# A strided sparse attention followed by an ELU layer: batch 2 transposed by the DMA crossbar, its P v and sums in one matmul, constants of v written first

## The chip, the cores and the metric

The kernel runs on one core of a Trainium2 chip. The core has a matrix engine (TensorE, in the profile PE, with its weight loads shown apart as PEld), a vector engine (VectorE, DVE), a scalar engine for activations (ScalarE, ACT), a general engine (GpSimd, POOL) and a sync engine (SP). Each runs its own list of instructions in order; they wait for each other through semaphores. The DMA engines move data between the chip's memory and the on-chip memory; a transfer is issued by SP, ACT or POOL. The metric is the time of one launch on the device in microseconds (us), as the median of several executions.

## What is computed

Eight batches of eight heads, 576 tokens, 64 values a head. Heads 0 to 3 attend to the last 32 tokens ("local"), heads 4 to 7 to every 32nd earlier token ("strided"). What comes out goes through two dense layers (512 to 2048 to 512) with an ELU between them.

```python
scores = scale * np.matmul(q, k.transpose(0, 1, 3, 2))
rel = pos[:, None] - pos[None, :]
mask_local = (rel >= 0) & (rel < 32)
mask_strided = (rel >= 0) & (pos[None, :] % 32 == pos[:, None] % 32)
masks = np.stack([mask_local if h < H // 2 else mask_strided for h in range(H)], axis=0)
attn = softmax(np.where(masks, scores, -1e9))
x = (attn @ v).transpose(0, 2, 1, 3).reshape(B * S, H * D)        # 4608 x 512
h = x @ w_in                                                      # 4608 x 2048
g = np.where(h > 0.0, h, np.exp(np.minimum(h, 0.0)) - 1.0)
out = g @ w_out                                                   # 4608 x 512
```

## The kernel before

**Tiling.** The tokens of a batch are cut into 8 residues of 72 tokens for the strided heads, and into 6 blocks of 96 for the local ones. Two heads make a pair, so a batch has four pairs: 0 and 1 are local, 2 and 3 strided; each pair has two halves u of 288 columns. A *piece* is one (pair, half). The result of a batch goes, transposed, into `xT` (128 x 4 x columns), a ring of 2304 columns. The dense layers go over 18 blocks j of 256 columns. `l1(j, t)` makes 256 of the 2048 hidden values: eight matmuls (line 406), an exponential on ACT (413), and on DVE a minimum (420) and a maximum (421); a "B" variant does more of it on ACT (416). `l2(j, kk, part)` is four matmuls (463), a quarter of one output tile of 128 tokens; after the last quarter ACT copies the tile to `osb` (468) and SP stores it in several transfers (451).

**A piece of attention.** `piece_S` (line 279 on) multiplies transposed keys by transposed queries into `sc` (293), ACT takes the exponential (296), and DVE multiplies by the mask (298 strided, 304 local) into `pm`. Then P v is made in one of two ways. `mm_O2` and `tail_O2` (kinds "M" and "E", or "X" for both at once) form the sums of the rows by a matmul with a tile of ones (368, 374) and P v by matmuls with 64 columns of v (378); the tail is one logarithm and one exponential on ACT (385, 387) and one product on DVE (313, 317) for 128 partitions. `piece_O` (kind "O") has v next to a block of 64 ones, so the same matmul (345) gives P v and the sums; its tail is two logarithms on 64 partitions (348, 349), one exponential (351) and two products on 64 partitions. Batches 0, 1 and 2 are done in the first way, batches 3 to 7 in the second.

**Who transposes.** q and k have to be turned so that the 64 values of a head lie on partitions. In batches 0, 1 and 2 `piece_T` does this on PE with an identity (268, 270) into a PSUM tile of the pool `p_x`, followed by two copies (253). In batches 3 to 7 `dma_T` (169) has SP issue four DMA transposes a batch: `qs` and `ks` (strided heads), `kl` and `ql` (local heads). The results lie in `qsT`, `ksT`, `klT`, `qlT`, two of each, used by turns.

**Loads.** From batch 1 on all loads of q, k and v are issued by POOL, which also casts them: `load_str` (143) one transfer for the four strided heads of a tensor, `load_kl16` (125) four transfers, `load_vl16` (133, 134) eight, `load_vsx16` (138) four, and `load_ql16` one transfer of 1024-byte rows in batches 1 and 2 (115) and four of 128-byte rows from batch 3 on (119). There is one `qs` and one `ks`: the load of the next batch into them waits until the transposes of the batch before have read them. POOL keeps to its order, and a load also waits until the eighth load before it has landed.

**Constants of v.** `vlx` and `vsx`, two of each, hold v with blocks of ones between. `one_columns(i)` writes these ones on ACT (528), for i = 0 inside batch 0 and for i = 1 after batch 0, behind a memset of `vlx[1]` on DVE (558).

**Order.** Everything is written out by hand. Batch 0 runs with matmuls on a constant between its pieces ("f"). Then come the first two blocks of the first layer (`l1_wide` at 431 to 440, and `l1`), with the strided transposes of batch 1 between them. Batch 1 follows in a list of steps, in which "2" is one quarter of `l2`, "S4" a `piece_S`, "A5" and "B4" an `mm_O2`, "E4" a `tail_O2`, "T0" a `piece_T`, "v", "k", "x" loads, and "t" the strided transposes of batch 2. The main loop counts n over `l1(j, t)`, j from 2 on; `at(n, ...)` hangs the pieces of batches 2 to 7 into it, at places given by `SC`, and `l2_to(n + 10)` puts in the quarters of `l2`. The pools that matter: `p_x` has two wide PSUM tiles (scores, P v and transposes), `p_h` three (hidden values), `p_o` one (output), and there are three `osb`.

Of the kernel before, what the change touches and what calls it, by code (L numbers as in the profile page):

```python
# [17 lines left out]
D = 64  # L18
# [12 lines left out]
def kernel(  # L31
# [44 lines left out]
    vs = const([RS, HG, NS * D], BF16, "vs")  # L76

    qlb = [const([RP, 2, NS, 2 * D], BF16, f"qlb{i}") for i in range(2)]
    qld = [t.rearrange("p a s c -> p (a s c)").rearrange("p (h c) -> p h c", h=HG) for t in qlb]
    klb = [const([LQ, 2, LB, 2 * D], BF16, f"klb{i}") for i in range(2)]  # L80
    KLW = PRE + 2 * S
    KSW = 16 * RP + 48
# [28 lines left out]


    def load_ql16(b):
        if b < 3:
            nc.gpsimd.dma_start(out=qld[b % 2][0:RS],
                                in_=q[b, 0:HG].rearrange("h (p s) d -> p h (s d)", s=NS))
            return
        for h in range(HG):
            nc.gpsimd.dma_start(  # L119
                out=qlb[b % 2][0:RS, h // 2, :, (h % 2) * D:(h % 2 + 1) * D],  # L120
                in_=q[b, h].rearrange("(p s) d -> p s d", s=NS))

    def load_kl16(b):
        for h in range(HG):
            nc.gpsimd.dma_start(  # L125
                out=klb[b % 2][:, h // 2, :, (h % 2) * D:(h % 2 + 1) * D],
                in_=k[b, h].rearrange("(t p) d -> p t d", p=LQ))

    def load_vl16(b):
        for h in range(HG):  # L130
            x = v[b, h].rearrange("(t p) d -> p t d", p=LQ)
            t = vlx[b % 2][:, h // 2, :, 2 * (h % 2) * D:(2 * (h % 2) + 1) * D]
            nc.gpsimd.dma_start(out=t[PRE:128], in_=x)  # L133
            nc.gpsimd.dma_start(out=t[0:PRE, 1:], in_=x[LQ - PRE:, 0:LB - 1, :])  # L134

    def load_vsx16(b):
        for h in range(HG):
            nc.gpsimd.dma_start(  # L138
                out=vsx[b % 2][:, h // 2, :, 2 * (h % 2) * D:(2 * (h % 2) + 1) * D],
                in_=v[b, HG + h].rearrange("(p s) d -> p s d", s=NS))  # L140

    def load_str(b, dst, src):
        nc.gpsimd.dma_start(  # L143
            out=dst[0:RS], in_=src[b, HG:2 * HG].rearrange("h (p s) d -> p h (s d)", s=NS))
# [35 lines left out]
    ones = const([128, D], BF16, "ones")  # L180
    dist = const([RS, RS], I32, "dist")
    nc.vector.memset(warm, 1.0)  # L182
    nc.vector.memset(identity, 1.0)
    nc.vector.memset(base_l, 1.0)
    for t in (qs, ks):
# [2 lines left out]
        identity, identity, compare_op=ALU.is_equal, fill=0.0,  # L188
        base=0, pattern=[[1, 128]], channel_multiplier=-1,
    )  # L190
    load_str(0, qs, q)
    load_str(0, ks, k)
    nc.gpsimd.affine_select(
# [37 lines left out]


    def pitch(b):
        return RS if b < 3 else RP

    def t_parts(b, hp, nm):
        i, a, n = b % 2, hp % 2, RS
        if hp >= 2:
            src = qs if nm == "q" else ks
            dst = (qsT if nm == "q" else ksT)[i][:, a * 8 * n:(a + 1) * 8 * n]  # L240
            blk = [src[0:n, 2 * a + j // 4, (j % 4) * 128:(j % 4 + 1) * 128] for j in range(8)]
        elif nm == "q":
            dst = qlT[i][:, a * 8 * n:(a + 1) * 8 * n]
            blk = ([qlb[i][0:n, a, j] for j in range(NS)] if b not in (1, 2) else
                   [[qld[i][0:n, 2 * a + x, j * D:(j + 1) * D] for x in range(2)]
                    for j in range(NS)])
        else:
            dst = klT[i][:, PRE + a * S:PRE + (a + 1) * S]
            blk = [klb[i][:, a, j] for j in range(LB)]
        return dst, blk  # L250
# [4 lines left out]
    def piece_T(b, hp, engs=None, wide=True):  # L255
        both = [t_parts(b, hp, nm) for nm in "qk"]
        if wide:
            pw = p_x.tile([128, 2, 1024], BF16, tag="x", name="tp2")
            ps = [pw[:, 0, 0:S], pw[:, 1, 0:S]]
        else:  # L260
            ps = [p_h.tile([128, S], BF16, tag="h", name="tp") for _ in range(2)]
        for i, (dst, blk) in enumerate(both):
            n = S // len(blk)
            for j, x in enumerate(blk):
                o = ps[i][:, j * n:(j + 1) * n]
                if type(x) is list:
                    for z in range(2):
                        nc.tensor.transpose(o[z * D:(z + 1) * D], x[z], identity[0:n, 0:n])
                else:
                    nc.tensor.transpose(o, x, identity[0:n, 0:n])  # L270
        for i, (dst, blk) in enumerate(both):
            copy(engs[i] if engs else nc.vector, dst, ps[i])

# [248 lines left out]
    cast_q(nc.vector, 1)  # L522
    cast_k(nc.vector, 1)
    P = [(p, u) for p in range(4) for u in range(2)]
    def one_columns(i):
        for t in (vlx[i], vsx[i]):
            o = t.rearrange("p a t (y d) -> p (a t) y d", d=D)[:, :, 1, :]
            nc.scalar.copy(o, warm[0:o.shape[0], 0:D].unsqueeze(1).to_broadcast(o.shape))

    for it in ("f7 S0 S1 1 f6 T1 f6 S2 S3 m f8 T2 T3q T3k f3 S4 S5 f3 S6 S7 M4 f3 E4 M5 f3 E5 M6 f3 E6 "  # L530
               "v M7 f3 E7 M0 f3 E0 M1 f3 E1 M2 f3 E2 M3 f12 E3").split():
        n = int(it[1:].strip("qk")) if len(it) > 1 else 0
        if it == "m":
            mask_strided()
        elif it[0] == "f":
            spins(n)
        elif it == "1":
            one_columns(0)
        elif it == "v":
            cast_v(nc.vector, 0, 0)  # L540
            cast_v(nc.gpsimd, 0, 1)
        elif it[0] == "T" and len(it) == 3:
            dst, blk = t_parts(0, n, it[2])
            ps = p_h.tile([128, S], BF16, tag="h", name="tp")
            for j, x in enumerate(blk):
                nc.tensor.transpose(ps[:, j * RS:(j + 1) * RS], x, identity[0:RS, 0:RS])
            copy(nc.vector, dst, ps)
        elif it[0] == "T":
            piece_T(0, n, (nc.vector, nc.scalar if n > 1 else nc.vector), False)
        elif it[0] == "S":  # L550
            do(("S", 0, *P[n]))
        elif it[0] == "M":
            do(("M", 0, *P[n], p_h))
        else:
            do(("E", 0, *P[n]))

    nc.vector.memset(qlb[1][64:RP], 0.0)
    nc.vector.memset(vlx[1][0:PRE, :, 0, :], 0.0)
    one_columns(1)
    load_str(1, qs, q)  # L560
    load_str(1, ks, k)

# [19 lines left out]
            l1(j, 4 * h + 3)  # L582
    load_str(2, qs, q)
    load_str(2, ks, k)
    load_kl16(2)
    load_ql16(2)
    load_vl16(2)


    L2S = [(j, kk, part) for j in range(NSUB) for kk in range(2) for part in range(4)]  # L590
# [8 lines left out]
                l2_last(j, kk)  # L599
            l2n[0] += 1  # L600

    for it in ("2 S4 2 S5 2 2 B4 S6 2 E4 A5 S7 2 E5 B6 2 E6 A7 2 E7 v "
               "T0 2 S0 S1 2 T1 k B0 2 E0 S2 2 A1 E1 S3 2 B2 E2 2 A3 2 E3 t 2 x").split():
        n = int(it[-1]) if it[-1].isdigit() else 0
        if it == "2":
            l2_to(l2n[0] + 1)
        elif it == "v":
            load_str(2, vs, v)
        elif it == "k":
            load_kl16(3)  # L610
            load_ql16(3)
            load_vsx16(3)
        elif it == "t":
            for p in (2, 3):
                piece_T(2, p)
        elif it == "x":
            load_str(3, qs, q)
            load_str(3, ks, k)
            load_vl16(3)
        elif it[0] == "T":  # L620
            piece_T(1, n, (nc.vector, nc.scalar))
        elif it[0] in "AB":
            do(("M", 1, *P[n], p_x if it[0] == "A" else p_h))
        else:
            do((it[0], 1, *P[n]))
# [3 lines left out]
    def at(n, *its):  # L629
        jobs.setdefault(int(2 * n) / 2, []).extend(its)  # L630

    def Ts(b):
        for w in ("qs", "ks", "kl", "ql"):
            dma_T(b, w)


    SC = {2: (2.5, 5.5, 9, 12), }
    SC.update({b: tuple(15 + 16 * (b - 3) + 4 * i for i in range(4)) for b in range(3, B)})
    for p, n in ((0, 8), (1, 10)):
        at(n, lambda p=p: do(("TT", 2, p)))  # L640

    for b in range(3, B):
        st = int(SC[b][0])
        if b > 3:
            at(st - 13, lambda b=b: (load_str(b, qs, q), load_str(b, ks, k), load_kl16(b),
                                     load_ql16(b), load_vsx16(b), load_vl16(b)))
        at(st - (3 if b == 3 else 4), lambda b=b: Ts(b))
    for b in range(2, B):
        for i, p in enumerate((2, 3, 0, 1)):
            for u in range(2):  # L650
                at(SC[b][i] + (.5 * u if b == 2 else 0), lambda b=b, p=p, u=u: do(("S", b, p, u)))
                at(SC[b][i] + 1.5 + .5 * u,
                   lambda b=b, p=p, u=u: do(("X" if b == 2 else "O", b, p, u)))

    L1S = [(j, t) for j in range(2, NSUB) for t in range(8)]
    for n, (j, t) in enumerate(L1S):
        for f in jobs.pop(n, []):
            f()
        l2_to(n + 10)
        for f in jobs.pop(n + .5, []):  # L660
            f()
        l1(j, t, mode="B" if n < 18 and n % 3 == 0 else "A")
# [31 lines left out]
```

The softmax here doesn't subtract the row's maximum and nothing guards it: scores larger than these inputs give would overflow.

## Time and profile before

| what | value |
|---|---|
| median of 7 executions | 324.29 us (323.62 to 325.37) |
| the profiled execution | 325.37 us |
| its span in the profile | 323.6 us |
| granted clock of TensorE, mean | 0.997 |
| POOL's DMA queue, share of 16 engines' span | 60.9% |
| SP's DMA queue, share of 16 engines' span | 24.2% |
| POOL's wait for the transposes of `qs` (4 times) | 48.7 us |
| PE's waits over 1 us | 1.3 us each, for: DVE g (421), ACT klT (253), DVE pm (298), DVE warm (182) |

The page gives each engine's busy time and its share of the span; then the span in 40 slices of 8.1 us with a digit for each engine (9 is 90% or more busy). The chain of waits follows the work back from the last instruction to what released it. The groups by line give a count, a mean time of one instruction in ns, and the idle time before. A busy matrix engine isn't one at its peak: matmuls overlap, so a group of eight of them is counted from the start of one to the start of the next group.

### The profile page before, as it was taken

To read this page: it belongs to the slowest core of one execution; us is meant where nothing else is said; L and a number is where in the kernel's file an instruction comes from. 1 tells how busy PE (TensorE), PEld (TensorE's weight loads), DVE (VectorE), ACT (ScalarE), POOL (GpSimd) and SP (SyncE) were. 2 spreads that over 40 slices of the span, in tenths; PEclk is the share of its full clock that TensorE was granted. 3 is DMA by queue.
4 is the path that set the end of the run, shared out by engine and by line. 5 is a ranking of instruction groups with operands and counts; after the bars stand their busy time and mean duration, and the time that the engine had idled before them with its cause. 6 is when DMAs were issued, how large, how long until landed. Compare 5 with 4: busy or idle time off the path is not lost.

```text
span 323.6 us, 7819 instructions
## 1 busy us (share of the span) xinstructions
PE 310.2 (96%) x2992; PEld 223.7 (69%) x2992; DVE 240.2 (74%) x485; ACT 220.2 (68%) x429; POOL 115.2 (36%) x162
## 2 busy tenths in 40 slices
PE   7889998989999999999999999999999999999995
PEld 5658854567667777777677777777777777777763
DVE  7664983477667888888888888888888866666660
ACT  3687766767678878878777887777778644444431
POOL 6362367897036912592179035820000000000000
PEclk9999999999999999999999999999999999999998
DMA  8999999999299949996999499978211111111212
GB/s 159 188 199 210 207 145 138 164 151 135 31 142 184 121 55 165 177 114 82 144 178 137 69 148 163 142 85 160 65 35 34 33 34 32 33 34 47 52 32 65
DMA packets 113990, 36.36 MB, mean 112 GB/s; under 512 B 101154, under 2 KB 107458, under 8 KB 113954
## 3 DMA queue, kind: packets, MB, share of 16 engines
q0 software_dynamic: 79696, 18.87, 60.9%
q1 hardware_dynamic: 32766, 16.28, 24.2%
q10 hardware_dynamic: 1492, 0.74, 1.0%
q8 instruction: 23, 0.38, 0.5%
q14 instruction: 13, 0.11, 0.1%
HBM read 38.04 MB, written 9.44 MB: 147 GB/s over the span
## 4 chain that ended last, share of the span: by engine, by line
PE 83%; DVE 6%; DMA 5%; ACT 3%; issue 2%; POOL 0%; DVEq 0%; SPq 0%; ACTq 0%
PE ops L463 36%; PE hps L406 34%; PE sc L293 3%; PE ox L345 3%; DMA ks<-in_k_dram 3%; DVE g L421 2%; DMA ksT<-ks 2%; PE opl L478 1%; DVE g L440 1%; DVE he L420 1%; PE tp L270 1%; PE idle L487 1%; PE o_ps L378 1%; PE hpw L431 1%; PE s_ps L368 0%
## 5 line engine op out<-in xcount | busy, mean ns | idle before, releaser
L463 PE MATMUL ops<-w_out_sb,g 128*128 128x512 bf16 x560 | 143.6, 380 | 0.1
L406 PE MATMUL hps<-xT,w_in_sb 128*128 128x256 bf16 x1088 | 140.6, 273 | 1.3 <-DVE g L421 1.3
L406 PEld LDWEIGHTS <-w_in_sb 128*128 128x128 bf16 x1088 | 117.3, 113 | 23.6 <-issue 1.5
L413 ACT ACTIVATE he<-hps 128x512 f32<-128x512 f32 x136 | 80.2, 592 | 52.3 <-PE hps L406 50.5
L421 DVE TENSOR_TENSOR g<-he,hps 128x512 bf16<-128x512 bf16 x130 | 89.4, 688 | 13.5
L463 PEld LDWEIGHTS <-g 128*128 128x128 bf16 x560 | 50.4, 98 | 37.2 <-DVE g L421 0.3
L420 DVE TENSOR_SCALAR he<-he 128x512 bf16<-128x512 f32 x130 | 58.6, 451 | 21.2 <-ACT he L413 19.8
L296 ACT ACTIVATE e<-sc 128x576 bf16<-128x576 f32 (+1 forms) x64 | 38.4, 645 | 4.8 <-PE sc L293 4.8
L468 ACT COPY osb<-ops 128x512 f32<-128x512 f32 x35 | 20.5, 587 | 12.4 <-PE ops L463 10.2
L143 POOL DMA_DIRECT2D qs<-in_q_dram x8 | 6.4, 805 | 49.9 <-DMA qsT<-qs 48.7
L125 POOL DMA_DIRECT2D klb<-in_k_dram x28 | 20.7, 751 | 8.1 <-DMA w_in_sb<-in_moe_w_in_dram 5.0
L348 ACT ACTIVATE ln<-ox 64x288 f32<-64x288 f32 x40 | 16.3, 408 | 10.5 <-PE ox L345 10.0
L133 POOL DMA_DIRECT2D vlx<-in_v_dram x28 | 21.8, 779 | 4.5 <-DMA w_out_sb<-in_moe_w_out_dram 2.1
L317 DVE TENSOR_TENSOR xT<-ox,rc 64x288 bf16<-64x288 f32 x40 | 18.1, 454 | 5.8 <-ACT rc L351 5.5
L313 DVE TENSOR_TENSOR xT<-ox,rc 64x288 bf16<-64x288 f32 x40 | 18.1, 454 | 5.2 <-ACT rc L351 4.9
L119 POOL DMA_DIRECT2D qlb<-in_q_dram x20 | 16.4, 827 | 13.2 <-DMA ks<-in_k_dram 9.1
L134 POOL DMA_DIRECT2D vlx<-in_v_dram x28 | 17.4, 621 | 4.7 <-DMA w_out_sb<-in_moe_w_out_dram 1.7
L351 ACT ACTIVATE rc<-ln 128x288 f32<-128x288 f32 x40 | 17.7, 443 | 1.3
L138 POOL DMA_DIRECT2D vsx<-in_v_dram x20 | 16.2, 815 | 0.7 <-issue 0.7
L349 ACT ACTIVATE ln<-ox 64x288 f32<-64x288 f32 x40 | 16.1, 403 | 0.5
L304 DVE TENSOR_TENSOR pm<-e,mask_l 128x576 bf16<-128x576 bf16 x32 | 13.5, 453 | 3.3 <-ACT e L296 3.0
L487 PE MATMUL idle<-warm 128*128 128x256 bf16 x92 | 14.2, 298 | 1.3 <-DVE warm L182 1.3
(101 smaller groups left out, 243.3 us busy)
## 6 DMA issues: line engine op xcount, KB each, us to landing
out_dram<-osb SPq DMA_DIRECT2D x31, 144.0 KB
qs<-in_q_dram POOLq DMA_DIRECT2D x8, 288.0 KB, 6.5
ks<-in_k_dram POOLq DMA_DIRECT2D x8, 288.0 KB, 8.8
w_in_sb<-in_moe_w_in_dram POOLq DMA_DIRECT2D x2, 1024.0 KB, 17.1
w_out_sb<-in_moe_w_out_dram POOLq DMA_DIRECT2D x4, 512.0 KB, 16.0
klb<-in_k_dram POOLq DMA_DIRECT2D x28, 72.0 KB, 8.3
vlx<-in_v_dram POOLq DMA_DIRECT2D x28, 72.0 KB, 3.7
qlb<-in_q_dram POOLq DMA_DIRECT2D x20, 72.0 KB, 6.1
```

The costliest lines, as they stand in the source:

```text
L125: nc.gpsimd.dma_start(out=klb[b % 2][:, h // 2, :, (h % 2) * D:(h % 2 + 1) * D], in_=k[b, h].rearrange("(t p) d -> p t d", p=LQ))
L133: nc.gpsimd.dma_start(out=t[PRE:128], in_=x)
L296: nc.scalar.activation(e[0:R], sc[0:R, :, 0:W], ACT.Exp, scale=scale)
L313: nc.vector.tensor_mul(xs[:, u * W:(u + 1) * W], o[pr], rc[pr])
L317: nc.vector.tensor_mul(dst, o[pr].rearrange(pat, b=3, s=NS), rc[pr].rearrange(pat, b=3, s=NS))
L351: nc.scalar.activation(rc, ln, ACT.Exp, scale=-1.0)
L406: nc.tensor.matmul(hps[:, mm], lhsT=w_in_of(m, c), rhs=xT[:, c, r0:r0 + SUB], start=(c == 0), stop=(c == KC - 1))
L413: nc.scalar.activation(e, hps, ACT.Exp)
L420: eng.tensor_scalar(e1, e, scalar1=1.0, scalar2=1.0, op0=ALU.min, op1=ALU.subtract)
L421: nc.vector.tensor_tensor(gt, e1, hps, op=ALU.max)
L463: nc.tensor.matmul(ops, lhsT=g[:, m, kk * 128:(kk + 1) * 128], rhs=w_out_sb[:, m, :], start=(m == 0), stop=(m == MC - 1))
L468: nc.scalar.copy(o_sb, ops)
```

## The change

Batch 2 gets the form of batches 3 to 7: four DMA transposes instead of `piece_T`, kind "O" instead of "X", `vsx` instead of `vs`, and the padded pitch of 80. q of batches 1 and 2 is loaded in four transfers like that of the others, and batch 1's `piece_T` transposes two heads at once. The columns of ones, for both buffers, and the memset of `vlx[1]` move to the start. The loads of batch 2 stand at "v" and those of batch 3 at "k" and "x", in another order. Three quarters of `l2` move from the list of batch 1 into the first steps of the main loop. The transposes of batch 3 are issued at n = 11 (strided) and 15 (local) instead of all at 12.

```diff
     def load_ql16(b):
-        if b < 3:
-            nc.gpsimd.dma_start(out=qld[b % 2][0:RS],
-                                in_=q[b, 0:HG].rearrange("h (p s) d -> p h (s d)", s=NS))
-            return
         for h in range(HG):
...
     nc.vector.memset(warm, 1.0)
+    nc.vector.memset(vlx[1][0:PRE, :, 0, :], 0.0)
     nc.vector.memset(identity, 1.0)
...
+    def one_columns(i):
+        for t in (vlx[i], vsx[i]):
+            o = t.rearrange("p a t (y d) -> p (a t) y d", d=D)[:, :, 1, :]
+            nc.scalar.copy(o, warm[0:o.shape[0], 0:D].unsqueeze(1).to_broadcast(o.shape))
+
+    for i in range(2):
+        one_columns(i)
     load_str(0, qs, q)
     load_str(0, ks, k)
...
     def pitch(b):
-        return RS if b < 3 else RP
+        return RS if b < 2 else RP
...
-            blk = ([qlb[i][0:n, a, j] for j in range(NS)] if b not in (1, 2) else
-                   [[qld[i][0:n, 2 * a + x, j * D:(j + 1) * D] for x in range(2)]
-                    for j in range(NS)])
+            blk = [qlb[i][0:n, a, j] for j in range(NS)]
...
-                if type(x) is list:
-                    for z in range(2):
-                        nc.tensor.transpose(o[z * D:(z + 1) * D], x[z], identity[0:n, 0:n])
-                else:
-                    nc.tensor.transpose(o, x, identity[0:n, 0:n])
+                nc.tensor.transpose(o, x, identity[0:n, 0:n])
...
     nc.vector.memset(qlb[1][64:RP], 0.0)
-    nc.vector.memset(vlx[1][0:PRE, :, 0, :], 0.0)
-    one_columns(1)
     load_str(1, qs, q)
...
     load_str(2, qs, q)
     load_str(2, ks, k)
-    load_kl16(2)
-    load_ql16(2)
-    load_vl16(2)
...
-    for it in ("2 S4 2 S5 2 2 B4 S6 2 E4 A5 S7 2 E5 B6 2 E6 A7 2 E7 v "
-               "T0 2 S0 S1 2 T1 k B0 2 E0 S2 2 A1 E1 S3 2 B2 E2 2 A3 2 E3 t 2 x").split():
+    for it in ("2 S4 2 S5 2 2 B4 S6 2 E4 A5 S7 2 E5 B6 2 E6 A7 v 2 t E7 T0 2 S0 S1 2 T1 k B0 2 E0 S2 2 A1 E1 S3 t B2 2 "
+               "E2 A3 E3 x").split():
...
         elif it == "v":
-            load_str(2, vs, v)
+            load_vsx16(2)
+            load_kl16(2)
+            load_ql16(2)
+            load_vl16(2)
         elif it == "k":
+            load_str(3, qs, q)
+            load_str(3, ks, k)
+            load_vsx16(3)
             load_kl16(3)
             load_ql16(3)
-            load_vsx16(3)
         elif it == "t":
-            for p in (2, 3):
-                piece_T(2, p)
+            Ts(2, *(("qs", "ks") if l2n[0] < 10 else ("kl", "ql")))
         elif it == "x":
-            load_str(3, qs, q)
-            load_str(3, ks, k)
             load_vl16(3)
         elif it[0] == "T":
-            piece_T(1, n, (nc.vector, nc.scalar))
+            piece_T(1, n, (nc.vector, nc.scalar if n else nc.vector))
...
-    for p, n in ((0, 8), (1, 10)):
-        at(n, lambda p=p: do(("TT", 2, p)))
...
-        at(st - (3 if b == 3 else 4), lambda b=b: Ts(b))
+        at(st - 4, lambda b=b: Ts(b, "qs", "ks"))
+        at(st - (0 if b == 3 else 4), lambda b=b: Ts(b, "kl", "ql"))
...
-                   lambda b=b, p=p, u=u: do(("X" if b == 2 else "O", b, p, u)))
+                   lambda b=b, p=p, u=u: do(("O", b, p, u)))
...
-        l2_to(n + 10)
+        l2_to(max(n + 10, min(13 + (n + 2) // 2, 16)))
```

`Ts(b, names)` calls `dma_T` for each name.

More of the change, by code (lines that the diff above doesn't have):

```diff
@@ L78 @@
     qlb = [const([RP, 2, NS, 2 * D], BF16, f"qlb{i}") for i in range(2)]
-    qld = [t.rearrange("p a s c -> p (a s c)").rearrange("p (h c) -> p h c", h=HG) for t in qlb]
     klb = [const([LQ, 2, LB, 2 * D], BF16, f"klb{i}") for i in range(2)]
@@ L524 @@
     P = [(p, u) for p in range(4) for u in range(2)]
[L525 to L530, printed above, removed]
+    for it in ("f7 S0 S1 f6 T1 f6 S2 S3 m f8 T2 T3q T3k f3 S4 S5 f3 S6 S7 M4 f3 E4 M5 f3 E5 M6 f3 E6 "
                "v M7 f3 E7 M0 f3 E0 M1 f3 E1 M2 f3 E2 M3 f12 E3").split():
@@ L536 @@
             spins(n)
-        elif it == "1":
-            one_columns(0)
         elif it == "v":
@@ L600, in l2_to, with Ts @@
             l2n[0] += 1
-    for it in ("2 S4 2 S5 2 2 B4 S6 2 E4 A5 S7 2 E5 B6 2 E6 A7 2 E7 v "
-               "T0 2 S0 S1 2 T1 k B0 2 E0 S2 2 A1 E1 S3 2 B2 E2 2 A3 2 E3 t 2 x").split():
+    def Ts(b, *names):
+        for w in names:
+            dma_T(b, w)
+    for it in ("2 S4 2 S5 2 2 B4 S6 2 E4 A5 S7 2 E5 B6 2 E6 A7 v 2 t E7 T0 2 S0 S1 2 T1 k B0 2 E0 S2 2 A1 E1 S3 t B2 2 "
+               "E2 A3 E3 x").split():
         n = int(it[-1]) if it[-1].isdigit() else 0
@@ L630, in at @@
         jobs.setdefault(int(2 * n) / 2, []).extend(its)
-    def Ts(b):
-        for w in ("qs", "ks", "kl", "ql"):
-            dma_T(b, w)
     SC = {2: (2.5, 5.5, 9, 12), }
     SC.update({b: tuple(15 + 16 * (b - 3) + 4 * i for i in range(4)) for b in range(3, B)})
-    for p, n in ((0, 8), (1, 10)):
-        at(n, lambda p=p: do(("TT", 2, p)))
     for b in range(3, B):
```

## The prediction

> **What bounds the kernel now.** I read the page first: engine totals, then the slices for DMA.
>
> ```profile
> PE 310.2 (96%) x2992; PEld 223.7 (69%) x2992; DVE 240.2 (74%) x485; ACT 220.2 (68%) x429; POOL 115.2 (36%) x162
> ...
> DMA  8999999999299949996999499978211111111212
> ```
>
> PE is the bound, 13.4 us short of the whole span, and DMA is nearly full in the first 70 us. The busy time by stage tells where the rest lies (columns: stage, its length, then busy time of PE, PEld, DVE, ACT and POOL, clock, DMA share, GB/s).
>
> ```profile
> 25.40:42.10 16.70, 15.33 (x162) 14.89 (x161) 12.04 (x21) 12.68 (x17) 5.00 (x7) 1.00 1.18 207
> 42.10:66.50 24.40, 22.76 (x270) 11.54 (x269) 13.21 (x29) 14.85 (x31) 18.84 (x28) 1.00 1.37 145
> 66.50:80.00 13.50, 12.07 (x162) 9.49 (x161) 9.89 (x20) 11.84 (x24) 11.97 (x16) 1.00 1.71 146
> 80.00:96.70 16.70, 16.50 (x170) 10.58 (x168) 11.57 (x24) 11.31 (x23) 2.79 (x5) 1.00 0.66 88
> 96.70:245.00 148.30, 147.80 (x1427) 107.84 (x1427) 127.43 (x258) 118.16 (x243) 62.95 (x86) 1.00 1.05 122
> ```
>
> After 96.7 us PE has almost no idle time, and its work there stays. So the change is worth what it brings forward PE's arrival at batch 3; that lead is kept to the end. Three waits in the earlier stages matter. First ACT, in order of time (start, duration, what, idle before):
>
> ```profile
> 26.96 0.83 ACT L528 COPY vlx<-warm 128x768 bf16<-128x768 bf16 x1 [2.02 <-DVE vlx L558]
> 27.70 1.04 ACT L528 COPY vsx<-warm 72x1024 bf16<-72x1024 bf16 x1
> 28.64 1.01 ACT L437 ACTIVATE big<-hpw 128x1024 f32<-128x1024 f32 x1
> ```
>
> The constants stand in front of the first exponential of the dense layers. Then PE, where a piece of batch 2 waits for the mask product, and the chain of waits, with a copy of transposed keys in front of batch 1's scores:
>
> ```profile
> 72.80 0.31 PE L368 MATMUL so<-pm,ones 72*64 72x288 bf16 x2 [1.29 <-DVE pm L298]
> ```
>
> ```profile
> 54.92 0.65 ACT klT L253
> 55.56 0.05 issue
> 55.61 0.43 PE sc L293 x12
> ```
>
> Last, what a DMA transpose takes. SP and POOL in order of time, and the chain of waits later:
>
> ```profile
> 88.27 1.45 SPq L169 DMA_TRANSPOSE qsT<-qs  x1
> 89.84 1.89 SPq L169 DMA_TRANSPOSE ksT<-ks  x1
> ```
>
> ```profile
> 95.25 0.72 POOL L143 DMA_DIRECT2D ks<-in_k_dram  x1 [0.54 <-DMA ksT<-ks]
> ```
>
> ```profile
> 154.98 5.90 DMA ksT<-ks
> ```
>
> From issue to landing `ksT` takes 95.25 - 89.84 = 5.4 us and 5.9 us, both with POOL's loads at rest, and the second one holds the chain.
>
> **The constants.** PE's first wide product starts at 25.40 and takes 1.91, so ACT could begin at 27.34 instead of 28.64: 1.30 saved. DVE's first maximum moves from 30.60 to 29.30, DVE then works without a break until 46, and PE's stop of 1.33 before 33.01 (hidden values not yet freed by line 421) goes. The four copies now at the start cost 2 x (0.83 + 1.04) = 3.74: from the end of the table load at 2.08 they end near 5.8, before the cast at 6.10 that waits 4.01 for k. That wait hides them with 0.3 to spare; past it each 0.1 would delay the first transposes by 0.1. The memset of 0.22 goes ahead of DVE's memsets of `qs` and `ks`, for which POOL's first two loads wait, and the chain runs through the second (9.15 us from 4.00). Nothing hides it: 0.2 lost (0 to 0.45 if the 0.25 of issue time seen ahead of such a memset comes again). Net +1.1.
>
> **PE's work.** Removed: 32 transposes at 64.67, 1.18; pairs 0 and 1 at 79.41 and 84.59, 0.64 each, 1.28; 16 half transposes of batch 1's q (0.38 becomes 0.26 a pair), 0.25; sums by ones, 8 x 0.13 (71.07 to 71.19, 86.20 to 86.34), 1.0. The joint matmuls take 0.26 a piece against 0.24: -0.1. Sum 3.6. On DVE the eight copies that go (0.45 each, 3.6) pay for the eight more products (0.45, 3.6). ACT gets 8 x 0.42 = 3.4 more logarithms, less 0.65 for T0's copy, which goes to DVE.
>
> **Waits that go.** The 1.29 at 72.80, since a quarter of `l2` (0.97) now stands between the two pieces and another ahead of the first scores; 0.3 at 55.6 (copy of 0.38 on DVE for 0.65 on ACT); 0.2 at 82.16 (copies of transposes). Sum 1.8.
>
> **Waits that come.** I walk the engines in order with the spacings of these rows. (a) With one quarter of `l2` less behind S3, A3's mask product comes 1.9 after S3's scores (ACT has E1 first, then 0.65, then DVE 0.46), while PE has 0.37 + 0.97 of work: 0.5. (b) Block 2 needs the last result of batch 1, 1.5 after A3 (63.63 to 65.12: logarithm, exponential, product); one quarter of `l2` (0.87) covers it where 2.9 us of work did: 0.6. So `l1(2, 0)` starts at 62.9 instead of 66.55, still owing two quarters of `l2`. (c) From n = 4 on ACT is serial: relu to 69.2, a tail of 1.2, the output copy 0.55, a tail of 1.2. The next scores need the PSUM tile that is free when the first tail's two products end, at 71.3; PE is there at 70.55, so 0.75, then 0.5 at n = 6, 0.4 and 0.3 at n = 7, 0.4 at n = 12: 2.3. If ACT kept up it would be 0; by the full 3.4 more on ACT it would be 3.4. Sum 3.4. Together: 1.1 + 3.6 + 1.8 - 3.4 = 3.1 gained, if data is in time.
>
> **Loads and crossbar.** POOL waits for the load eight places back. Three more transfers for batch 1's q (0.81 each) put the load of `qs`(2) at 50.0 instead of 47.86 and `ks`(2) at 50.75. With 7.8 from issue to landing (the same load before; 7.1 to 8.8 in other rows) `ks` lands near 58.6, say 59.2 since an output store now runs beside it. SP stands at `qsT` until about 57 and issues `ksT` at 59.2. Under POOL's loads no row shows a transpose's landing cleanly. From below 4.7 (123.16 to POOL's wait end at 127.90). From above double, 9.4: loads of `klb` take 4.6 at 62.7 to 64.9 and 8.3 at 96.0 to 98.1, right behind transposes. I take 7.5, nearer the upper end, for POOL is loading all the while: landed at 66.7. The first scores of batch 2 stand at 65.6 + 0.2 on PE: a wait of about 1.0 (0 to 2.9). All later work is behind it on PE, so it counts in full.
>
> Behind the waiting transposes on SP stand the output stores, for which ACT's copy would wait; with three `osb` and the first store landed by 50 us that costs nothing, and one store time, 3 to 6 us, if it were one buffer. `kl` and `ql`: POOL issues `vsx` (4 x 0.81), `klb` and `qlb` until about 63; landing 5 later, transposes 7.5 later, 75.5 (80 by the upper ends); pair 0's scores stand at 80.2. Covered, barely at the upper end. Batch 3's loads come after POOL's last of batch 2, about 69, where they ran from 62.7 to 80.2 before; needed at n = 11 and 15, past 85 us. Hidden.
>
> One rule speaks against the four small q transfers. The Trainium skill, "DMA: Bandwidth & Descriptors", Specifications, wants at least 512 B for line rate, and a read-modify-write below. These rows disagree: four `klb` loads of 128-byte rows, 72 KB each, land within 2.2 + 4.2 - 4.9 = 1.5 us of each other, while the 288 KB of `ks` in 1024-byte rows land 1.9 after `qs`. An estimate from that page, each small row written twice, would put batch 1's and 2's q some 2 us later each, and the sum 1 to 2 us worse.
>
> Another rule speaks against the move itself: "VectorE: DVE Perf Modes", Rules for kernel authors, prefers TensorE for a 128x128 transpose where PSUM will do. Here 32 PE transposes took 1.18 us, 37 ns each, on the engine that is the bound; by the rule the 2.5 us of batch 2 would have stayed there.
>
> **The sum.** 3.1 - 1.0 = 2.1 to 2.2. The span of 323.6 becomes 321.45. The profiled execution, with 1.77 around its span, is the slowest of the seven; set against the median, 324.29 - 2.2 = 322.1 us.
>
> **Rivals.** (1) The crossbar is in time and no wait comes: 324.29 - 3.1 = 321.2, to 320.2 if ACT's waits of (c) are half of mine. For it speaks 4.7; against it DMA's share of 1.37 to 1.71 in this stretch. (2) Slower: `ksT` lands late. The gain is used up when it lands at 65.8 + 3.1 = 68.9, and the kernel is slower from 69.6. With `ks` landing 8.8 after issue, one issue of 1.9 on SP behind `qsT`, and 9.4 for the crossbar it is 50.75 + 8.8 + 1.9 + 9.4 = 70.9: a wait of 5.1, 324.29 + 2.0 = 326.3. For it: everything is serial, load, SP, crossbar, PE, and `ksT` already holds the chain at 154.98. Against: it takes the upper end three times. (3) The move doesn't pay in the stretch: ACT, busy 11.84 of 13.50 at 66.5 to 80, takes its full 3.4 and the wait is 1.7, so only about 0.3 is left: 324.0.
>
> **How the numbers follow.** Forecast 322.1, chance 0.55, its own range 321.4 to 323.5; rival (1) 0.15, (2) 0.20, (3) 0.10. A measurement can't tell changes within 0.2% (0.65 us) from none. Faster: 0.55 + 0.15 = 0.70; same: 0.10; slower 0.20. The range reaches down into (1) to 320.4 and up past (3) to 325.0, leaving most of (2) out.
>
> **What would show it.** Right: the first wide exponential near 27.5; `l1(2, 0)` near 63; PE's wait for DMA `ksT` of about 1 us near 66; waits of scores in `p_x` for the products at 313 between 70 and 76; PE full from there on. Wrong: a wait for `ksT` over 3 us, a wait for `klT` or `qlT`, the first cast of k later than 6.3, or PE idle after batch 3 has begun, which would mean that loads of later batches have slipped.

## The result, and the profile after

| what | before | after |
|---|---|---|
| median of all executions | 324.46 us (64 runs, 323.31 to 327.30) | 327.95 us (27 runs, 325.18 to 331.70) |
| ratio of the two, 95% interval | | 1.0087 [1.0071, 1.0103] |
| the profiled execution | 325.37 us | 326.04 us |
| its span | 323.6 us | 324.2 us |

The change makes the kernel slower by 0.9%, some 2.8 us; forecast were 322.1 us, and a range to 325.0. The ratio is of fast executions: it leaves out two slow ones of the changed kernel (330.55 and 331.70 us), which the medians in the table hold. Line numbers of the changed kernel are lower by 3 to 5 in the lines spoken of here; the copies of the constants stand at 190. Below, the engine totals from the page of the changed kernel.

```profile
PE 306.7 (95%) x2884; PEld 221.9 (68%) x2884; DVE 241.4 (74%) x486; ACT 222.5 (69%) x436; POOL 123.0 (38%) x171
```

PE has 3.5 us less to do and yet a span 0.6 longer: the work went, and about 4 us of idle time came. The busy times of four stages, with the columns and limits used before, tell where:

```profile
25.40:42.10 16.70, 16.44 (x172) 15.15 (x171) 13.26 (x21) 11.96 (x17) 5.63 (x7) 1.00 1.21 206
42.10:66.50 24.40, 20.88 (x220) 11.18 (x218) 12.38 (x28) 14.74 (x31) 19.48 (x27) 1.00 1.56 135
66.50:80.00 13.50, 9.35 (x115) 7.04 (x116) 8.19 (x17) 10.16 (x21) 10.08 (x14) 1.00 1.67 184
80.00:96.70 16.70, 15.68 (x147) 10.87 (x145) 12.81 (x26) 14.02 (x31) 10.90 (x15) 1.00 1.43 125
```

The first stage has gained 1.1 us of PE work (15.33 before). ACT's rows show why: the copies are done ahead of the cast, which still waits for its data, and the first wide exponential starts at 26.96 instead of 28.64. Of these 1.68 us the change makes 1.3: PE's first wide product itself began 0.39 earlier in this execution (25.01 for 25.40), and from there to the exponential it is 1.95 us instead of 3.24.

```profile
2.10 0.83 ACT L190 COPY vlx<-warm 128x768 bf16<-128x768 bf16 x1
...
5.97 0.83 ACT L147 CAST klb<-kl 96x768 bf16<-96x768 f32 x1 [0.42 <-DMA kl<-in_k_dram]
...
26.96 1.02 ACT L434 ACTIVATE big<-hpw 128x1024 f32<-128x1024 f32 x1 [2.45 <-PE hpw L428]
```

From 42.1 to 80 PE stands idle for 7.7 us, where it was idle for 3.1. Its waits, from the timeline of PE (start, duration, what; in brackets the idle time before it and its releaser):

```profile
62.65 1.80 PE L403 MATMUL hps<-xT,w_in_sb 128*128 128x256 bf16 x15 [0.39 <-DVE xT L314]
...
68.50 0.30 PE L290 MATMUL sc<-qsT,ksT 64*128 64x72 bf16 x8 [3.19 <-DMA ksT<-ks]
...
74.58 0.31 PE L290 MATMUL sc<-qsT,ksT 64*128 64x72 bf16 x8 [1.18 <-DVE xT L310]
...
76.37 0.31 PE L290 MATMUL sc<-qsT,ksT 64*128 64x72 bf16 x8 [0.49 <-ACT e L293]
...
77.95 0.42 PE L342 MATMUL ox<-pm,vsx 72*128 72x72 bf16 x8 [0.28 <-DVE pm L295]
...
79.44 0.42 PE L342 MATMUL ox<-pm,vsx 72*128 72x72 bf16 x8 [0.21 <-DVE pm L295]
...
91.08 0.30 PE L290 MATMUL sc<-qlT,klT 64*128 64x96 bf16 x6 [0.87 <-DVE xT L314]
...
98.02 0.31 PE L290 MATMUL sc<-qsT,ksT 64*128 64x72 bf16 x8 [1.42 <-DVE xT L314]
```

Two things stand out. The first scores of batch 2 wait 3.19 us for the transposed keys. Then, up to the second scores of batch 3 at 98.02, come six waits of 4.45 us in all, called the waits behind the tails from here on: scores that wait for a piece's last product (310, 314) or once for an exponential (293), or P v that waits for a mask product (295) behind such a tail. Before, the stretch from 72.9 to 98 had one wait of 0.20. What held the keys is seen on SP, and in the chain of waits:

```profile
55.22 2.19 SPq L164 DMA_TRANSPOSE qsT<-qs  x1
57.53 4.68 SPq L164 DMA_TRANSPOSE ksT<-ks  x1
```

```profile
57.53 10.92 DMA ksT<-ks
```

The keys were loaded and their transpose was issued at 57.5, earlier than the 59.2 that I had reckoned. From SP's issue to landing the transpose took 10.9 us.

### The profile page after: what moved, and what is told of

Read it like the earlier page. It is cut to its first block, busy times and chain, and to the rows that moved or that the text cites. A ratio compares the mean times of both kernels' runs of the same rounds, so it can differ in the third digit from the quotient of the medians.

```text
span 324.2 us, 7648 instructions
## 1 busy us (share of the span) xinstructions
PE 306.7 (95%) x2884; PEld 221.9 (68%) x2884; DVE 241.4 (74%) x486; ACT 222.5 (69%) x436; POOL 123.0 (38%) x171
## 4 chain that ended last, share of the span: by engine, by line
PE 81%; DMA 6%; DVE 6%; ACT 3%; issue 2%; POOL 0%; DVEq 0%; ACTq 0%
PE ops L460 35%; PE hps L403 33%; PE ox L342 3%; DMA ksT<-ks 3%; PE sc L290 3%; DMA ks<-in_k_dram 3%; PE hpw L428 2%; PE idle L484 1%; DVE g L418 1%; DVE xT L314 1%; PE opl L475 1%; DVE he L417 1%; DVE g L437 1%; PE tp L267 1%; PE o_ps L375 1%
## 5 line engine op out<-in xcount | busy, mean ns | idle before, releaser
L114 POOL DMA_DIRECT2D qlb<-in_q_dram x28 | 23.5, 843 | 16.1 <-DMA ks<-in_k_dram 9.8
L310 DVE TENSOR_TENSOR xT<-ox,rc 64x288 bf16<-64x288 f32 x48 | 21.8, 454 | 7.7 <-ACT rc L348 7.3
L314 DVE TENSOR_TENSOR xT<-ox,rc 64x288 bf16<-64x288 f32 x48 | 21.8, 453 | 7.4 <-ACT rc L348 7.1
L345 ACT ACTIVATE ln<-ox 64x288 f32<-64x288 f32 x48 | 19.6, 408 | 10.7 <-PE ox L342 10.0
L348 ACT ACTIVATE rc<-ln 128x288 f32<-128x288 f32 x48 | 21.3, 443 | 1.5
L133 POOL DMA_DIRECT2D vsx<-in_v_dram x24 | 19.4, 813 | 6.1 <-PE hps L403 2.8
L346 ACT ACTIVATE ln<-ox 64x288 f32<-64x288 f32 x48 | 19.3, 403 | 0.6
L295 DVE TENSOR_TENSOR pm<-e,mask_s 72x576 bf16<-72x576 bf16 x32 | 13.5, 449 | 5.3 <-ACT e L293 5.0
```

The lines of the kernel that those rows point to most:

```text
L114: nc.gpsimd.dma_start(out=qlb[b % 2][0:RS, h // 2, :, (h % 2) * D:(h % 2 + 1) * D], in_=q[b, h].rearrange("(p s) d -> p s d", s=NS))
L310: nc.vector.tensor_mul(xs[:, u * W:(u + 1) * W], o[pr], rc[pr])
L314: nc.vector.tensor_mul(dst, o[pr].rearrange(pat, b=3, s=NS), rc[pr].rearrange(pat, b=3, s=NS))
L348: nc.scalar.activation(rc, ln, ACT.Exp, scale=-1.0)
```

## The experiments

Eleven variants ran, each against the kernel before on the same chip (its medians there were 324.31, 324.14 and 325.52 us in three sessions), so that the ratios are to be compared. One per cent is 3.24 us. The changed kernel itself ran in other sessions, and so did some partners of the comparisons below.

| run | ratio to before, 95% interval | median, us |
|---|---|---|
| const_alone | 0.9971 [0.9948, 0.9993] | 323.42 |
| joint_pv_alone | 1.0131 [1.0109, 1.0154] | 328.86 |
| strided_on_pe | 1.0038 [1.0011, 1.0065] | 325.27 |
| qs_ks_earlier | 0.9980 [0.9951, 1.0009] | 323.30 |
| twostep_pv_crossbar | 0.9992 [0.9964, 1.0021] | 324.16 |
| early_ks_twostep_pv | 0.9874 [0.9837, 0.9912] | 321.11 |
| pe_kept_busy | 1.0048 [1.0027, 1.0069] | 326.40 |
| pool_loads_held | 1.0123 [1.0065, 1.0182] | 328.58 |
| one_log_of_two | 0.9911 [0.9876, 0.9946] | 322.27 |
| one_product_of_two | 0.9912 [0.9881, 0.9943] | 322.26 |
| early_ks_v_split | 0.9944 [0.9912, 0.9975] | 323.58 |

### const_alone: the constants at the start, nothing else

The kernel before, with the memset and `one_columns` at the start as in the diff of the change, and the two later calls taken out.

> The kernel before with the constants of v alone moved to the start. If the front saves what the prediction said (1.3 us less 0.2), the time falls by about 1.1 us, to 323.4; the first wide exponential on ACT starts near 27.2 instead of 28.64. If the saving at the front is lost again before batch 3, the time stays within 0.3 us of before. If the copies at the start cost more than they save, it rises.

Measured 0.9971, 0.9 us gained. This part does what was reckoned for it.

### joint_pv_alone: the joint P v alone

```diff
-            load_str(2, vs, v)
+            load_vsx16(2)
...
-                   lambda b=b, p=p, u=u: do(("X" if b == 2 else "O", b, p, u)))
+                   lambda b=b, p=p, u=u: do(("O", b, p, u)))
```

> The kernel before with batch 2's P v and sums in joint matmuls (vsx loaded, kind O) and its transposes left on PE. Theory A (the late crossbar is the whole loss): no change or a gain of up to 1 us from the 1.0 us of sums that PE no longer makes. Theory B (the serial tail on ACT and the two wide PSUM tiles give the gain back): slower than before by 1 to 3 us, with PE waiting for the products at line 313 and 317 before later scores.

Measured 1.0131: 4.2 us lost, with batch 2 still transposed on PE, and more than the 1 to 3 us of theory B. From 71 to 100 us PE's waits sum to 5.6 us in this run's profile, 1.5 before. Two of them in the timeline of PE (lines are numbered as before):

```profile
73.98 0.31 PE L293 MATMUL sc<-qsT,ksT 64*128 64x72 bf16 x8 [0.70 <-DVE xT L313]
...
99.54 0.31 PE L293 MATMUL sc<-qsT,ksT 64*128 64x72 bf16 x8 [1.42 <-DVE xT L317]
```

These waits, and one of 0.73 between them at 92.60, are at the places of the changed kernel's, the last as long to the hundredth. They need no crossbar.

### strided_on_pe: the strided transposes of batch 2 back on PE

```diff
+        elif it == "p":
+            for p in (2, 3):
+                piece_T(2, p)
         elif it == "t":
-            Ts(2, *(("qs", "ks") if l2n[0] < 10 else ("kl", "ql")))
+            Ts(2, "kl", "ql")
```

Here `"p"` stands before `"x"` in the list of steps, the first `"t"` is taken out, and the strided heads keep the pitch of 72. The loads of batch 3 that stood at `"k"` move to `"x"`, since `qs` and `ks` are read until then.

> The kernel after, but the strided heads of batch 2 transposed on PE again (32 transposes, 1.2 us, and four copies on DVE), so nothing waits for the DMA transpose of ks in batch 2; its local heads stay with the crossbar. Theory A: the wait of 3.2 us goes for 1.2 us of PE work and the kernel is 2 to 3 us faster than the one after, 322 to 323 if no clock is lost. Theory B: PE's waits behind the tails (4.4 us in the profile after) stay, and the time is not below 324.

Measured 1.0038 against the changed kernel's 1.0087: the wait for `ksT` is gone and 1.6 us come back, not the whole 3.2. PE has 1.2 us more work for the transposes, it waits 0.84 us for a product of batch 1 between them, and its clock fell twice in the profiled execution (columns of the stages, the clock third from the end; then PE's timeline):

```profile
60.00:65.00 5.00, 3.61 (x47) 2.24 (x45) 3.37 (x8) 2.09 (x5) 5.00 (x8) 0.83 1.91 162
...
75.00:80.00 5.00, 4.50 (x40) 3.15 (x36) 4.25 (x9) 3.83 (x8) 4.28 (x6) 0.69 2.14 175
```

```profile
62.94 0.42 PE L267 MATMUL tp<-identity,qs 72*128 72x72 bf16 x8 [0.84 <-DVE xT L314]
```

### qs_ks_earlier: the crossbar given more time

```diff
-    load_vl16(1)
...
     load_str(2, qs, q)
     load_str(2, ks, k)
+    load_vl16(1)
...
-"2 S4 2 S5 2 2 B4 S6 2 E4 A5 S7 2 E5 B6 2 E6 A7 v 2 t E7 ..."
+"2 S4 2 S5 2 2 B4 S6 2 t E4 A5 S7 2 E5 B6 2 E6 A7 v 2 E7 ..."
```

> The kernel after with the loads of qs and ks of batch 2 ahead of the eight v loads of batch 1, and their transposes two pieces earlier on SP. ksT should land by 63 to 65 us instead of 68.4. Theory A: PE's wait for ksT goes (0 to 0.5 us) and the time falls by about 3 us from the one after, to 321 to 323. Theory B: the wait goes but most of it comes back as PE's waits for PSUM tiles held by tails on ACT, and the time is 323.5 or more. If v of batch 1 now lands too late, PE waits for it at the first local P v of batch 1, near 56 us.

Measured 0.9980, 1.07% below the changed kernel: the late keys cost it 3.5 us. On SP both transposes are issued some 4.6 us earlier, and the issue of the second is shorter; there is no wait for `ksT` left.

```profile
50.71 2.00 SPq L164 DMA_TRANSPOSE qsT<-qs  x1
52.82 2.92 SPq L164 DMA_TRANSPOSE ksT<-ks  x1
```

The waits behind the tails stay: six of 4.6 us (PE's timeline in this run, the longest):

```profile
94.59 0.31 PE L290 MATMUL sc<-qsT,ksT 64*128 64x72 bf16 x8 [1.42 <-DVE xT L314]
```

### twostep_pv_crossbar and early_ks_twostep_pv: the joint P v undone

In the changed kernel, and in that of qs_ks_earlier:

```diff
-            load_vsx16(2)
+            load_str(2, vs, v)
...
-                   lambda b=b, p=p, u=u: do(("O", b, p, u)))
+                   lambda b=b, p=p, u=u: do(("X" if b == 2 else "O", b, p, u)))
```

> The changed kernel with the P v of batch 2's strided heads back in two steps (matmuls of their own for the sums, then for the values, as before the change); the crossbar's transposes, their places and the constants stay. Theory A (the late ksT costs the time, the joint P v nothing worth speaking of): the wait of S(2,2,0) on ksT stays near 3 us, PE has some 1.5 to 2 us more work, the median is 327 to 330. Theory B (the joint P v's serial tail on ScalarE and VectorE costs what the joint_pv_alone run showed, 4.5 us): the waits behind the tails (4.45 us summed over six rows in the changed kernel) fall under 2, the ksT wait stays, the median falls to 324.5 to 326.

> Both repairs together: the loads and the crossbar transposes of batch 2's strided heads earlier, as in the qs_ks_earlier run (323.3), and the two-step P v for batch 2. If the tails' waits are worth their sum in that run's profile (4.6 us in six rows) less the PE work that the two-step form adds (some 2 us), 320.5 to 322, ahead of both kernels. If PE runs into ScalarE's work instead (exponentials and copies that are as many as before), 323 to 324 and the waits only change their names.

Measured 0.9992 and 0.9874. Each is about 1% below its partner with the joint form (1.0087 and 0.9980): that form costs 0.95% and 1.06%, 3.1 and 3.4 us net of the matmuls that it saves. And the late keys cost 1.07% with it and 1.18% without it. The two losses add up. In the profile of twostep_pv_crossbar PE still waits for the keys, and the waits behind the tails are gone:

```profile
67.50 0.30 PE L290 MATMUL sc<-qsT,ksT 64*128 64x72 bf16 x8 [2.83 <-DMA ksT<-ks]
```

early_ks_twostep_pv, with both undone, is 4.1 us faster than the kernel before, the best of this study. Its stages show PE nearly full where the changed kernel had its holes:

```profile
66.50:80.00 13.50, 12.82 (x146) 9.05 (x146) 10.38 (x21) 11.00 (x24) 11.24 (x16) 1.00 1.59 168
80.00:96.70 16.70, 16.54 (x165) 11.35 (x167) 10.76 (x22) 13.56 (x29) 12.45 (x18) 1.00 1.38 137
```

### one_log_of_two and one_product_of_two: what in the tail costs it

Both start from qs_ks_earlier, and change `piece_O` for batch 2. Their results are not the reference's: each leaves out a part of the tail for half of the heads.

```diff
+        if b == 2:
+            nc.scalar.activation(rc[lo], ln[lo], ACT.Exp, scale=-1.0)
+            x_out(b, hp, u, lo, o[0], rc)
+            x_out(b, hp, u, hi, o[1], mask_l[:, 0:3].rearrange("p b s n -> p (b s n)"))
+            return
         nc.scalar.activation(ln[hi], o[1][lo], ACT.Ln)
```

```diff
+        if b == 2:
+            x_out(b, hp, u, slice(0, 128), o[1], rc)
+            return
         x_out(b, hp, u, lo, o[0], rc)
```

> The version of the qs_ks_earlier run (323.3 us, ratio 0.998; joint P v, no wait for ksT) with one logarithm of the two left out in each of batch 2's eight pieces; the heads of one of each two are multiplied by a constant tile instead of their reciprocal sums, so their values are not the reference's. Products, matmuls, transfers stay. Theory L (the second logarithm on ScalarE, 0.42 a piece, is what makes PE wait behind the tails, 4.6 us in six rows): the waits of scores for xT fall by 2 or more, the time to 320.5 to 322. Theory V (the second product on VectorE does it): the time stays within 0.7 of 323.3 and the rows for xT stay.

> The same version with the two products on 64 partitions of each of batch 2's pieces replaced by one product on 128 partitions that reads one PSUM half, so half the heads' values are not the reference's; both logarithms stay. Theory V: the time falls to 320.5 to 322 and the waits for xT fall by 2 or more. Theory L: the time stays within 0.7 of 323.3. If both this run and the other gain 1 to 1.5 us, the tail as a whole is the price and its two parts share it.

Both gain, 0.69% and 0.68% on qs_ks_earlier by the ratios, some 2.2 us each, and are no different from each other. Their intervals just miss that of qs_ks_earlier. But the kernel before was 1.2 us slower in their session (325.52 us, 324.31 in that of qs_ks_earlier), and by the medians as they are (322.27 and 322.26 for 323.30) it is only 1.0 us: take 1 to 2.2. Neither theory stood alone: the logarithm and the product are in series between the last matmul of a piece and the moment its PSUM tile is free, and each takes 0.4 us eight times. The six waits fall from 4.6 us to 2.95 and 2.33. The last of them, 1.42 in qs_ks_earlier, in the run with one logarithm and in that with one product:

```profile
93.36 0.30 PE L290 MATMUL sc<-qsT,ksT 64*128 64x72 bf16 x8 [0.91 <-DVE xT L314]
```

```profile
93.24 0.31 PE L290 MATMUL sc<-qsT,ksT 64*128 64x72 bf16 x8 [0.32 <-DVE xT L314]
```

### pool_loads_held: why the crossbar took 10.9 us

```diff
-            Ts(2, *(("qs", "ks") if l2n[0] < 10 else ("kl", "ql")))
+            if l2n[0] < 10:
+                Ts(2, "qs", "ks")
+                load_str(3, ks, k)
+                load_vsx16(2)
+                load_kl16(2)
+                load_ql16(2)
+                load_vl16(2)
+            else:
+                Ts(2, "kl", "ql")
```

The loads named here are taken out at "v" and "k". The load of batch 3 into `ks` waits for the transpose, and holds all of POOL's queue. This variant ran four times.

> The changed kernel with GpSimd's later loads (k's batch 3, then vs, kl, ql and vl of batch 2) issued behind ksT instead of ahead of it, so that nothing of GpSimd's queue runs beside the two crossbar transposes. Theory E (they were slow, 10.9 us from issue, because the other loads shared the DMA engines): ksT takes 4.5 to 7 us from its issue, the wait of S(2,2,0) falls from 3.19 to 0 to 1 us. Theory F (two transposes one behind the other on SyncE take this long whatever else runs): 9.5 to 11 us, and the wait stays near 3. The time itself may rise, as batch 2's lower heads then come later.

SP's issue, and POOL's queue, whose next load starts when `ksT` has landed:

```profile
57.12 1.34 SPq L164 DMA_TRANSPOSE ksT<-ks  x1
```

```profile
62.36 0.71 POOL L138 DMA_DIRECT2D ks<-in_k_dram  x1 [11.56 <-DMA ksT<-ks]
```

Issue to release is 62.36 - 57.12 = 5.2 us with POOL's queue still, instead of 10.9, and the issue itself takes 1.34 on SP instead of 4.68. So it is the loads beside it that slow the transpose, not the second transpose behind the first. The wait of the first scores is gone; the time rose to 1.0123, since the local queries came late instead (PE's timeline):

```profile
83.65 0.30 PE L290 MATMUL sc<-qlT,klT 64*128 64x96 bf16 x6 [4.23 <-DMA qlT<-qlb]
```

### pe_kept_busy: does the wait cost more than its length?

```diff
+    def keep(n):
+        ps = p_h.tile([128, 256], F32, tag="h", name="keep")
+        for _ in range(n):
+            spin(ps)
+
+    at(2.5, lambda: keep(28))
```

The changed kernel's executions differ in the mean granted clock of TensorE. Of 28, the profiled one included, the 7 at 0.998 or more took 325.18 to 326.82 us, and the other 21, all at 0.995 or less, took 325.85 to 331.70; the kernel before was at 0.997 or more in 51 of the 69 that ran beside these experiments.

> The changed kernel with 28 matmuls that nothing reads, some 3 us of PE, put ahead of S(2,2,0), where PE waits 3.19 us for ksT. Theory D (part of the loss is TensorE's clock, which an idle PE brings down for stretches after the wait): the median goes down from 327.95 towards the 325.3 that the changed kernel shows at a granted clock of 0.999, its runs lie closer together and their clocks are 0.998 and more. Theory A alone (the wait costs its 3.2 us, the clock is chance): the median stays at 327 to 329 and the clocks spread as before.

```profile
64.89 3.22 PE L484 MATMUL keep<-warm 128*128 128x256 bf16 x28
68.91 0.30 PE L290 MATMUL sc<-qsT,ksT 64*128 64x72 bf16 x8 [0.80 <-DMA ksT<-ks]
```

The scores start 0.4 us later than in the changed kernel's profile, and still the kernel is faster: 1.0048, with an interval that just doesn't meet 1.0087's. Nine of 12 clocks are 0.998 or more. So some 1.3 us of the loss, the difference of the two ratios (0.4 to 2.1 by their intervals), is TensorE's clock, brought down by an idle PE. The clocks give nearly the same: 0.9943 on the mean of the 28 executions and 0.9977 on that of the 69 make (0.9977 - 0.9943) x 326 = 1.1 us, an estimate. The rest stays.

Which wait it is can be read from two other runs. twostep_pv_crossbar has the wait for the keys and none behind the tails, in the same session as pe_kept_busy: 3 of its 12 clocks are 0.997 or more. qs_ks_earlier has the waits behind the tails and none for the keys: 10 of 12. So the lower clock comes mostly with the wait for the keys.

### early_ks_v_split: a better version that wasn't

The longest wait left in early_ks_twostep_pv was 1.44 us for `vlx` of batch 1, so its first half goes ahead of the strided loads again.

```diff
+    load_vl16(1, (0, 1))
     load_str(2, qs, q)
     load_str(2, ks, k)
-    load_vl16(1)
+    load_vl16(1, (2, 3))
```

> The version of the early_ks_twostep_pv run (321.11 us) with batch 1's v of heads 0 and 1 loaded ahead of batch 2's qs and ks, and that of heads 2 and 3 behind. That run's longest wait was 1.44 us of a P v of batch 1's local heads for vlx, with ksT landed some 6 us before it is needed. If the wait goes and ksT is still in time, 319.5 to 320.5; if ksT's transpose is slowed again by the loads beside it, the wait comes back there and the time is 321 to 323.

Measured 0.9944, 2.3 us worse than without it. Four loads ahead of `qs` and `ks` moved the issue of `ksT` from 53.05 to 55.20, and its landing to 66.9; the chain of this run, and PE's timeline, have

```profile
55.20 11.72 DMA ksT<-ks
```

```profile
66.97 0.30 PE L290 MATMUL sc<-qsT,ksT 64*128 64x72 bf16 x8 [1.98 <-DMA ksT<-ks]
```

and the busy times in steps of 1 us show what happened to PE's clock after it:

```profile
67.00:68.00 1.00, 1.00 (x13) 0.76 (x14) 0.01 (x1) 0.65 (x1) 1.00 (x2) 0.66 1.47 267
68.00:69.00 1.00, 1.00 (x7) 0.47 (x7) 0.45 (x1) 0.00 (x0) 0.41 (x2) 0.50 2.58 210
69.00:70.00 1.00, 1.00 (x13) 0.72 (x13) 0.29 (x1) 0.92 (x2) 0.51 (x1) 0.50 1.92 122
70.00:71.00 1.00, 1.00 (x8) 0.58 (x6) 0.90 (x3) 0.21 (x1) 0.99 (x2) 0.63 1.26 133
```

PE is idle from 65.0 to 67.0, 1.98 us; then its clock (third from the end) is halved: (1 - 0.66) + 0.5 + 0.5 + (1 - 0.63) = 1.7 us of work lost, which at half speed is a stretch of 3.4 us. PE counts as fully busy the while. On either side of these four rows the clock is 1.00.

The same steps over the 13 profiled executions, from the start to 318 us, where PE's work nears its end, show six such stretches, each of 1.7 us lost:

| run | PE's wait just before | at half clock, some |
|---|---|---|
| early_ks_v_split | 1.98 for `ksT`, to 66.97 | 67.3 to 70.7 |
| twostep_pv_crossbar | 2.83 for `ksT`, to 67.50 | 68.2 to 71.6 |
| pool_loads_held | 4.23 for `qlT`, to 83.65 | 84.0 to 87.4 |
| one_log_of_two | 2.56 for `ksT` of a later batch, to 159.60 | 160.2 to 163.6 |
| strided_on_pe | 0.84 for a product of batch 1, to 62.94 | 63.3 to 66.7 |
| strided_on_pe | 1.18 and 0.50 behind the tails, to 76.57 | 77.0 to 80.3 |

The length of the wait doesn't settle it: 0.84 us was followed by half clock, and the 3.19 us of the changed kernel's profile were not. One stretch of 1.7 us is 0.005 of the span, and the runs with one here have a mean clock of 0.993 to 0.995, that with two 0.990.

## Why the prediction was wrong

**What held.** The constants: 1.1 reckoned, 0.9 measured. PE's work: 3.6 reckoned, 310.2 - 306.7 = 3.5 measured. The 1.29 us wait for the mask product is gone. The early walk, (a) and (b): 0.5 and 0.6 reckoned, 0.55 and 0.39 in PE's timeline. Block 2 began at 61.99 for the 62.9 given, but 0.39 of this lead was there at 25 us, before anything that the prediction prices, and 0.39 went in (b)'s wait after the first matmul. `klT` and `qlT` were in time.

**The crossbar, mis-sized.** I took 7.5 us from issue to landing and 9.4 as the upper end, from transposes with POOL's loads at rest and by doubling. It was 10.9, beyond the upper end, and the wait 3.19 for 1.0 reckoned. pool_loads_held shows the reason: the loads beside it, without which it took 5.2. The prediction's own sign of being wrong, a wait for `ksT` over 3 us, came. Rival (2) has this mechanism, but not by the road that it took: `ks` came early, and the crossbar alone took longer than the 9.4 that it allowed. `ksT` landed at 68.4, before the 68.9 that used up the gain and the 69.6 from which that rival counted a loss: by its count the late keys alone left some 0.5 us of gain.

**The tails, mis-sized.** Step (c) had 2.3 us; 4.45 came, above the 3.4 that I gave as its upper end. Four of the waits between 74 and 80 were met within 0.45 us each (0.75, 0.5, 0.4, 0.3 reckoned; 1.18, 0.49, 0.28, 0.21 measured). What I missed lies later: 0.87 for 0.4 at 91.08, and 1.42 at the second scores of batch 3, where I had PE full. The upper end counted the logarithms alone. The eight extra products I had balanced on DVE against eight copies that go; by busy time that is nearly right (240.2 before, 241.4 after), but the second product stands at the end of each piece's tail, behind both logarithms, and the scores at 91.08 and 98.02 wait for a product (314). The run with one product shows it: 1 to 2.2 us.

**A term left out.** The clock. Nothing in the prediction made a wait of PE dearer than its length; pe_kept_busy puts some 1.3 us of the 2.8 on that, and each stretch at half clock that a profile shows costs 1.7.

**The sum again.** With 2.2 more for the crossbar, 2.15 more for the tails and 1.3 for the clock, the predicted 322.1 become 327.75 us, against 1.0087 x 324.46 = 327.3 measured. The profiled execution, at a clock of 0.998, is one of the better ones; the median lies 1.9 above it. One slip in the prediction's sums changed nothing: half of (c) is 1.15, so rival (1) reaches down to 320.0 and not to 320.2. Rival (3) said that ScalarE eats the gain, and was right in kind: the joint form costs 3.1 to 3.4 us net, though not by ScalarE alone.

**The rule for TensorE** (the Trainium skill, "VectorE: DVE Perf Modes", Rules for kernel authors), which I had set against the move, fits the change as it was made: strided_on_pe is 0.5% faster than the changed kernel. With the loads earlier the crossbar is faster by another 0.6% (qs_ks_earlier), so the measurement sides with the move where there is time for it.

What stays open: why a wait is followed by half clock in one execution and not in another, whether the joint form cost more in the kernel before (4.2 us) than in the changed one (3.1 to 3.4), since the intervals overlap, and how the joint form would do with a shorter tail and all of its work in it, which no run had.

## What to carry to other kernels

A DMA transpose is priced with the loads that run beside it, from issue to landing, and is started before the loads that are needed later than it; two transfers moved by a few microseconds decided 3.5 us here. Taking work off the bounding engine can be worth less than nothing when it lengthens the chain that frees that engine's buffers, as the joint form did here: count the time from the last matmul to the free tile, not the busy time of the engines in between. And price a wait of the matrix engine above its own length: here some were followed by a stretch at half clock that cost another 1.7 us, and filling one with matmuls that nothing reads made the kernel 0.4% faster.

## What the hardware did that I had not expected

- The same crossbar transpose took from issue to landing, or to the release that marks it, 5.2 us with POOL's queue still and 10.9 and 11.7 us with its loads running; its issue held SP for 1.34 us or for 4.68.
- After waits of 0.84 to 4.23 us without a matmul TensorE ran at half its clock for some 3.4 us, six times in 13 profiled executions. In the changed kernel's own profile 3.19 us of idling left the clock at 1.00, so it doesn't come every time. The Trainium skill, "TensorE: Matmul & The Clock Gate", Why this matters for your kernels, warns of gaps over about 3 us; here shorter ones were enough.
